# The hand-over between the passes and the last part of a transformer block's forward and backward kernel, rearranged

## The chip, the cores and the metric

The kernel runs on one core of a Trainium2 chip. The metric is the device time of one execution in microseconds (us), given as the median of several executions. Beside it stands one profiled execution, from which all rows of the profile come. The engines are TensorE (PE; PEld is its weight load), VectorE (DVE), ScalarE (ACT), GpSimd (POOL) and SyncE (SP), which only issues DMA. Each works through its own queue in order, and they wait for each other by semaphores. GpSimd and ScalarE can issue DMA too.

## The reference

One transformer block, forward and backward: layer norm, then attention with 16 heads of width 28 and a gated feed-forward part side by side, both added to the input. The kernel returns the output and the gradients of the input and the five weights.

```python
def _fwd_reference(A_x, A_wqkv, A_wo, B_x, B_w_gate, B_w_up, B_w_down):
    def _A_ref(x, wqkv, wo):
        ...
        qkv = (x @ wqkv).reshape(B, S, 3, H, Dh) ...      # q, k, v per head
        scores = jnp.einsum("bhqd,bhkd->bhqk", q, k) * (Dh ** -0.5)
        p = _softmax(scores, axis=-1)
        o = jnp.einsum("bhqk,bhkd->bhqd", p, v)
        return ... o ... @ wo
    def _B_ref(x, w_gate, w_up, w_down):
        return (_silu(x @ w_gate) * (x @ w_up)) @ w_down
    xn = _layernorm(A_x, axis=-1)
    return A_x + _A_ref(xn, A_wqkv, A_wo) + _B_ref(xn, B_w_gate, B_w_up, B_w_down)

_out, _vjp = jax.vjp(_f, A_x, A_wqkv, A_wo, B_w_gate, B_w_up, B_w_down)
_grads = _vjp(grad_out)
```

Here S is 2048 tokens, D is 448, the feed-forward width 1792; everything is bf16. Two gradients matter for the change. The gradient of `wo` (dWo, `out_3`) is, for each head, the attention output transposed times `grad_out`. The gradient of the input (`out_1`) ends in the layer norm's backward step: with g the gradient that reaches the normalised input xn, each token's result is `grad_out + rstd * (g - mean(g) - xn * mean(g * xn))`. So it needs two sums over the 448 columns of a token, of g and of g times xn, before any of its values can be written.

## The kernel before

Tokens are cut into 16 tiles of 128, heads into 4 groups of 4 (one head per 32 partitions), queries into 4 chunks of 512.

**Forward part (`slot`, L523, to L627).** 256 slots, one for each group, query chunk and key tile: two score tiles on TensorE (L535, `s_ps`, three PSUM tiles in turn), two exponentials on ScalarE (L541, `eT`). What else TensorE has to do is cut into generators, called units, which yield after each matmul with a cost; `Fillers.pump` (L57) takes a budget of such cost per slot and places units between the slots. Units with a ready slot stand in `fill.first`: `o_unit` (L394) multiplies exponentials with values and adds up in `oacc`, `mid1` (L411) transposes and divides into `od`, `mid2` (L429) makes the gradient of the attention output and a chain of small VectorE steps (L442 to L451), whose results a DMA transpose and stores on SP carry to memory. `dwo_unit` (L459) makes a group's dWo: 16 matmuls (L462), one per token tile, over the `od` of its four query chunks, a copy to `dw_o` (L467) and four stores, one per head (L470). It becomes ready six slots after a group's last chunk. For the last group there is no slot left, so `fill.finish` (L627) runs the last `o_unit`, `mid1`, `mid2` and `dwo_unit` one after the other. Its stores are issued by ScalarE, those of the other groups by SP. `sp_flush` (L171) issues stores that were held back until their transposes are under way.

**Main backward part.** 512 steps, in each: scores again (`row`, L695, tile `sb`, a single one), the exponential (`ew`, L710, `e_sb`), the product with the upstream gradient (L703, `db`; L717 on VectorE, `ds_sb`), then the sums for dK and dV (`kv`, L745, L749) one or two steps later and, four steps at a time, transposes of `ds_sb` by DMA on SP (L720) and by TensorE (L731) for dQ. Other matmuls fill in. Operands come back from memory: `load_q(g, qc)` and `load_k` (L662 on) reserve a tile and put its loads into a list with due steps (`drip`, L640). GpSimd issues them from there: `drop` (L646) sends up to a budget of bytes per step, from step 2 on, each behind a one-column copy `pace` that waits for that step's `ds_sb` (L1055); `have` (L657) sends what is wanted at once. Before the first step L672 sends the first key and query chunk; query chunks 1 to 3 and the next keys go into the list. Step 4 is the first of query chunk 1.

**The last part (from L1081).** For each of 16 token tiles, `dx_a(t)` (L1095) adds the last terms of g on TensorE (`tok`, six PSUM tiles in turn). For an odd tile it also adds the sum so far, `dxg` in SBUF, by a matmul with the identity (L1099), and ScalarE writes a bf16 copy `gs` that nobody reads, for the sum of g on the way (L1107). For an even tile VectorE adds `dxg` itself and takes the sum (L1110). Then VectorE multiplies with xn and takes the second sum (`pr`, L1113), from PSUM for odd tiles. `dx_b(t)` (L1116) scales both sums (two VectorE instructions on 128x1, L1120), makes the first half of the result on ScalarE (L1123, from PSUM for odd tiles), the second on VectorE (L1126, tile `e_sb`), adds them on GpSimd (L1128, `dx`) and stores on SP (L1129). The loop (L1146) does `dx_a(t)` and `dx_b(t - 1)` in each turn, and one unit of the list `rest`: two units of transposes of dV or dK (`dsp_unit`, L825), four of dQ (`dsq_unit`, L1138, copied by ScalarE at L1140), four of dWqkv (`dwq_unit`, L838: 16 matmuls each that need all of `dsp`, copies on ScalarE and VectorE at L844 to L847, a store on GpSimd).

The order in which a queue holds its instructions is the order in which the code emits them.

Of the kernel before, what the change touches and what calls it, by code (L numbers as in the profile page):

```python
# [8 lines left out]
ACT = mybir.ActivationFunctionType  # L9
ALU = mybir.AluOpType  # L10
AX = mybir.AxisListType
FP32 = mybir.dt.float32
BF16 = mybir.dt.bfloat16
# [4 lines left out]
D = 448  # L18
H = 16
DH = 28  # L20
F = 1792
G = 4
HP = 32
NT = S // 128
NFC = F // 128
P = 128
# [9 lines left out]
def pv(hh):  # L36
    return (hh + 2) % 4
# [50 lines left out]
def kernel(  # L88
# [23 lines left out]
    PE, DVE, ACTE, POOL, SP = nc.tensor, nc.vector, nc.scalar, nc.gpsimd, nc.sync  # L112
# [14 lines left out]
    xn_sp = xn_t[:, :NT * D].rearrange("p (t d) -> p t d", d=D)  # L127
    rstd = const.tile([P, NT], FP32)
# [16 lines left out]
    ps_s = fwd.enter_context(tc.tile_pool(name="ps_s", bufs=3, space=PSUM))  # L145
    gen = fwd.enter_context(tc.tile_pool(name="gen", bufs=2, space=PSUM))
# [24 lines left out]
    def sp_flush():  # L171
        for o, i in late:
            SP.dma_start(out=o, in_=i)
        late.clear()
# [114 lines left out]
    def run(u):  # L289
        for _ in u:  # L290
            pass
# [102 lines left out]
    def o_unit(g, qc, m, eTs):  # L394
        ps = gen.tile([P, 512], FP32, name="gen")
        for kt in range(4 * m, 4 * m + 4):
            for hh in range(4):
                r = HP * pv(hh)
                PE.matmul(ps[r:r + HP, :], lhsT=VS[g][:, kt, r:r + HP], rhs=eTs[kt][hh // 2][:, hh % 2, :],  # L399
                          start=(kt % 4 == 0), stop=(kt % 4 == 3), tile_position=(0, r), skip_group_check=True)  # L400
            if kt % 4 < 3:
                yield 216
        if m == 0:
            oacc[g, qc] = wk.tile([P, 512], FP32, name="oacc")
            DVE.tensor_copy(out=oacc[g, qc][:], in_=ps[:])
        else:
            DVE.tensor_tensor(out=oacc[g, qc][:], in0=ps[:], in1=oacc[g, qc][:], op=ALU.add)
        o_done.add((g, qc, m))
        yield 316
# [47 lines left out]
        yield 60  # L457

    def dwo_unit(g):  # L459
        ps = gen.tile([P, 512], FP32, name="gen")  # L460
        for t in range(NT):
            PE.matmul(ps[:, :D], lhsT=od[g, t // 4][0][:, 0, t % 4, :], rhs=dy_sp[:, t, :],  # L462
                      start=(t == 0), stop=(t == NT - 1))
            if t < NT - 1:
                yield 189
        o = wk.tile([P, D], BF16, name="dw_o", bufs=1)
        DVE.tensor_copy(out=o[:], in_=ps[:, :D])  # L467
        for hh in range(4):
            h = g * 4 + hh
            (ACTE if g == G - 1 else SP).dma_start(out=out_3[h * DH:(h + 1) * DH, :], in_=o[HP * pv(hh):HP * pv(hh) + DH, :])  # L470
        yield 189

    fill = Fillers()
# [45 lines left out]
    NS = G * 4 * NT  # L519
# [3 lines left out]
    def slot(i):  # L523
        nonlocal eTs
        g, qc, kt = i // 64, (i // 16) % 4, i % 16
        qsl = slice(qc * 512, (qc + 1) * 512)
        m = i - EB // 2
        if m >= 0 and m % 4 == 0:
            fill.until(lambda: (m // 64, (m // 16) % 4, (m % 16) // 4) in o_done, i)
        sp2 = []  # L530
        for hp in range(2):
            s_ps = ps_s.tile([P, 2, 512], FP32, name="s_ps")
            for j in range(2):
                r = HP * (2 * hp + j)
                PE.matmul(s_ps[:, j, :], lhsT=KK[g][r:r + HP, kt * P:(kt + 1) * P], rhs=QQ[g][r:r + HP, qsl],  # L535
                          start=True, stop=True, tile_position=(r, 0))
            sp2.append(s_ps)
        e2 = []
        for hp in range(2):
            eT = wk.tile([P, 2, 512], BF16, name="eT", bufs=EB)  # L540
            ACTE.activation(out=eT[:], in_=sp2[hp][:], func=ACT.Exp, scale=SCALE)  # L541
            e2.append(eT)
        eTs[kt] = e2
        if kt % 4 == 3:
            fill.first.append((i + 1, lambda e=dict(eTs): o_unit(g, qc, kt // 4, e)))
        if kt == 15:
            fill.first.append((i + 3, lambda: mid1(g, qc)))
            fill.first.append((i + 4, lambda: mid2(g, qc)))
            if qc == 3:
                fill.first.append((i + 6, lambda: dwo_unit(g)))  # L550
            eTs = {}
        fill.pump(FWD_NS, i)
# [19 lines left out]
    for t in range(4):  # L572
        run(T_unit(xnT, xn_t, t, t % 2 == 0, ps_s if t < 2 else None))
    DVE.tensor_reduce(out=r_ones[:],
                      in_=ident_f[:].rearrange("p (a b) -> p a b", b=HP)[:, :, 28:30],
# [4 lines left out]
    proj(1, 0, True)  # L580
    proj(0, 0)
    slot(0)
    proj(2, 0)
    norm4(1)
    T(4, 5)
    slot(1)
    T(6, 7)
    proj(1, 1)
    stats4(2)
    slot(2)  # L590
    proj(2, 1)
    slot(3)
# [31 lines left out]
    slot(15)  # L624
    for i in range(16, NS):
        slot(i)
    fill.finish()  # L627
    sp_flush()
    fwd.close()

# [9 lines left out]
    def drip(key, pieces, due):  # L640
        slow.extend((due, key, o, i) for o, i in pieces)
        slow.sort(key=lambda x: x[0])
# [14 lines left out]
    def have(*keys):  # L657
        for x in [x for x in slow if x[1] in keys]:
            slow.remove(x)
            POOL.dma_start(out=x[2], in_=x[3])  # L660

    def load_q(g, qc):  # L662
        t = qside[g, qc] = bk.tile([P, 4, 512], BF16, name="qd", bufs=5)
        drip(("q", g, qc), [(t[:, i:i + 2], QD_d[g, qc, :, i:i + 2]) for i in (0, 2)], 128 * g + 4 * qc)
# [5 lines left out]
    load_k(0, 0)  # L670
    load_q(0, 0)
    have(("k", 0, 0), ("q", 0, 0))  # L672
    for qc in range(1, 4):
        load_q(0, qc)
    load_k(0, 1)

# [232 lines left out]
    dxs = {}  # L909
# [130 lines left out]
    for k in range(NB + 12):  # L1040
        now = k
        if k < NB:
            g, hp, kc, qc, qi = steps[k]
# [40 lines left out]
    tw, wqT = dxs["tw"], dxs["wq"]  # L1084
# [5 lines left out]
    SP.dma_start(out=dy2[1][:], in_=dy_d[:, 4:8, :])  # L1090
    dy4 = bk.tile([P, 8, D], BF16, name="dsT", bufs=3)
    SP.dma_start(out=dy4[:], in_=dy_d[:, 8:16, :])
    psd, sms = {}, {}

    def dx_a(t):  # L1095
        pst = ps_b.tile([P, 512], FP32, name="tok", bufs=6)
        ps = psd[t] = pst[:, :D]
        if t % 2:
            PE.matmul(ps, lhsT=ident_f[:], rhs=dxs["g"][:, t, :], start=True, stop=False)  # L1099
        for i, (l, r) in enumerate(last):  # L1100
            PE.matmul(ps, lhsT=l[:, t * P:(t + 1) * P], rhs=r, start=(i == 0 and t % 2 == 0), stop=(i == 3))  # L1101
        sa = tw.tile([P, 1], FP32, name="sa", bufs=4)
        sb = tw.tile([P, 1], FP32, name="sb", bufs=4)
        sms[t] = (sa, sb)
        if t % 2:
            gs = tw.tile([P, D], BF16, name="gs")
            ACTE.activation(out=gs[:], in_=ps, func=ACT.Identity, accum_out=sa[:])  # L1107
        else:
            psd[t] = dxs["g"][:, t, :]
            DVE.scalar_tensor_tensor(out=psd[t], in0=ps, scalar=1.0, in1=psd[t],  # L1110
                                     op0=ALU.mult, op1=ALU.add, accum_out=sa[:])
        pr = tw.tile([P, D], BF16, name="pr")
        DVE.scalar_tensor_tensor(out=pr[:], in0=psd[t], scalar=1.0, in1=xn_sp[:, t, :],  # L1113
                                 op0=ALU.mult, op1=ALU.mult, accum_out=sb[:])

    def dx_b(t):  # L1116
        ps = psd.pop(t)
        sa, sb = sms.pop(t)
        for x in (sa, sb):
            DVE.tensor_scalar(out=x[:], in0=x[:], scalar1=rstd[:, t:t + 1], scalar2=-1.0 / D,  # L1120
                              op0=ALU.mult, op1=ALU.mult)
        t1 = tw.tile([P, D], FP32, name="t1")[:]
        ACTE.activation(out=t1, in_=ps, func=ACT.Identity, scale=rstd[:, t:t + 1], bias=sa[:])  # L1123
        t2 = bk.tile([P, 512], FP32, name="e_sb", bufs=4)[:, :D]
        dy = dy2[t // 4][:, t % 4, :] if t < 8 else dy4[:, t - 8, :]
        DVE.scalar_tensor_tensor(out=t2, in0=xn_sp[:, t, :], scalar=sb[:], in1=dy, op0=ALU.mult, op1=ALU.add)  # L1126
        dx = tw.tile([P, D], BF16, name="dx")
        POOL.tensor_tensor(out=dx[:], in0=t1, in1=t2, op=ALU.add)  # L1128
        SP.dma_start(out=out1_d[:, t, :], in_=dx[:])  # L1129

    g = G - 1
    rest = [dsp_unit(g, 2, t8, "rest") for t8 in range(2)]
# [10 lines left out]

    rest += [dsq_unit(t4, "rest") for t4 in range(4)]
    rest += [dwq_unit(g, c, "rest") for c in range(4)]
    for t in range(NT + 1):  # L1146
        if t < NT:
            dx_a(t)
        if t > 0:
            dx_b(t - 1)  # L1150
        if rest:
            for _ in rest.pop(0):
                pass
    for u in rest:
# [35 lines left out]
```

## Time and profile before

| | before |
|---|---|
| median of 6 runs | 1594.11 us |
| lowest, highest run | 1585.56, 1622.87 us |
| profiled execution | 1602.12 us |
| its span | 1600.3 us |
| busy: TensorE, VectorE, ScalarE, GpSimd | 1362.6, 1191.1, 1148.7, 653.8 us |
| granted TensorE clock, mean | 0.962 |
| forward part, main part, last part | to about 669, 669 to 1546.6, 1546.6 to 1600.3 us of the span |

The profile is of one execution; a start is counted in us from the start of its span. A row of a timeline has start, length, engine, line, operation, what is written and read, how many instructions were merged, and in brackets how long the engine was idle before and what ended that. "q" behind an engine's name is its queue: an issue of DMA, not work. In a row of windows the columns are the stretch, its length, and the busy time of PE, PEld, DVE, ACT and POOL with the number of instructions, then the granted TensorE clock as a share of full speed, the busy share of DMA and GB/s. A group's row in the page has busy time and the mean of one instruction in ns. Line numbers are those of the kernel before, unless said otherwise.

### The profile page before, as it was taken

What the parts mean: (1) busy time and instruction counts of PE and PEld (TensorE: products, weight loads), DVE (VectorE), ACT (ScalarE), POOL (GpSimd) and SP (SyncE); (2) the same over time, 40 slices, a digit from 0 to 9 for tenths busy, and PEclk for the clock granted to TensorE, in tenths of its full rate; (3) what the DMA queues carried; (4) which work ended last, traced back from release to release, by engine and by line L of the source; (5) the groups of instructions that cost most, each with busy time, mean ns of one, the idle gap of its engine ahead of it and who ended that gap; (6) DMA issues with size and microseconds to landing.
All of it is one profiled execution on the core that took longest, in us unless ns stands there. A gap on an engine that the chain in (4) does not pass through costs nothing. (4 is left out here: it accounts for less than half of the span.)

```text
span 1600.3 us, 31339 instructions
## 1 busy us (share of the span) xinstructions
PE 1362.6 (85%) x11728; PEld 550.5 (34%) x11728; DVE 1191.1 (74%) x1603; ACT 1148.7 (72%) x1320; POOL 653.8 (41%) x1095
## 2 busy tenths in 40 slices
PE   5789888879889897677789889889899898988985
PEld 2333333323333333232333333323333333333332
DVE  7576556646665665287689998879889799969986
ACT  5588878868788887466567777757677777756753
POOL 3445344343434443045345634644524346141214
PEclk9899999999999999789889999999999999999998
DMA  4978856576667656289999998999979999899851
GB/s 126 198 187 196 184 136 154 130 182 150 146 164 169 158 145 137 71 176 178 161 202 220 226 184 177 185 223 201 223 140 193 162 209 227 159 161 184 160 126 45
DMA packets 652560, 270.42 MB, mean 169 GB/s; under 512 B 598600, under 2 KB 626648, under 8 KB 652408
## 3 DMA queue, kind: packets, MB, share of 16 engines
q1 hardware_dynamic: 626496, 198.85, 65.0%
q0 software_dynamic: 24336, 69.17, 17.2%
q8 instruction: 92, 1.51, 0.4%
q10 hardware_dynamic: 1576, 0.40, 0.1%
q14 instruction: 60, 0.49, 0.1%
HBM read 63.99 MB, written 58.85 MB: 77 GB/s over the span
## 5 line engine op out<-in xcount | busy, mean ns | idle before, releaser
L717 DVE TENSOR_TENSOR ds_sb<-db,e_sb 128x1024 bf16<-128x1024 f32 x512 | 623.2, 1222 | 107.3 <-PE db L703 37.3
L710 ACT ACTIVATE e_sb<-sb 128x1024 bf16<-128x1024 f32 x512 | 524.2, 1024 | 237.9 <-PE db L703 178.1
L541 ACT ACTIVATE eT<-s_ps 128x1024 bf16<-128x1024 f32 x512 | 491.9, 1026 | 115.5 <-PE s_ps L535 114.0
L695 PE MATMUL sb<-kd,qd 32*128 32x512 bf16 x1024 | 205.2, 391 | 71.5 <-ACT e_sb L710 56.2
L703 PE MATMUL db<-kd,qd 32*128 32x512 bf16 x1024 | 204.5, 394 | 5.1 <-DVE ds_sb L717 4.7
L331 POOL TENSOR_TENSOR nn<-nn,ag 128x512 f32<-128x512 f32 x56 | 71.1, 1269 | 285.4 <-DVE ag L329 284.5
L695 PEld LDWEIGHTS <-qd 32*128 32x128 bf16 x1024 | 74.7, 91 | 257.0 <-issue 239.4
L749 PE MATMUL acc<-ds_sb,qd 128*32 128x512 bf16 x1024 | 162.0, 395 | 1.1 <-DVE ds_sb L717 1.1
L796 POOL TENSOR_TENSOR dq_acc<-dq_acc,dq_st 128x512 f32<-128x512 f32 x88 | 111.8, 1271 | 123.3 <-ACT dq_st L795 121.9
L745 PE MATMUL acc<-e_sb,qd 128*32 128x512 bf16 x1024 | 161.3, 396 | 0.0
L1055 POOL COPY pace<-ds_sb 128x1 bf16<-128x1 bf16 x287 | 54.4, 189 | 207.1 <-DVE ds_sb L717 204.8
L535 PE MATMUL s_ps<-QQ,KK 32*128 32x512 bf16 x1024 | 112.3, 391 | 12.6 <-ACT eT L541 11.7
L946 PE MATMUL genb<-wguT,dau_c 128*128 128x448 bf16 x448 | 111.1, 358 | 4.8 <-DMA dau_c<-F_d 3.6
L731 PE MATMUL db<-ident_bf,ds_sb 128*128 128x128 bf16 x1088 | 85.6, 225 | 34.2 <-DVE ds_sb L717 27.6
L370 PE MATMUL gen<-xn_t,f_sp 128*128 128x448 bf16 x448 | 98.1, 356 | 9.8 <-DVE nn L346 5.4
L731 PEld LDWEIGHTS <-ds_sb 128*128 128x128 bf16 x1088 | 72.9, 100 | 62.4 <-issue 57.6
L370 PEld LDWEIGHTS <-f_sp 128*128 128x128 bf16 x672 | 60.4, 98 | 95.3 <-issue 34.5
L732 DVE COPY dsT<-db 128x1024 bf16<-128x1024 bf16 (+1 forms) x128 | 91.5, 715 | 1.0 <-PE db L731 1.0
L781 PE MATMUL genb<-dsT,kd 128*32 128x512 bf16 x1024 | 80.8, 389 | 2.1 <-DVE qd L791 1.2
L353 PE MATMUL gen<-dyT,wT_f 128*128 128x512 bf16 x224 | 63.6, 388 | 15.5 <-DVE nn L346 15.4
L535 PEld LDWEIGHTS <-KK 32*128 32x128 bf16 x1024 | 28.1, 91 | 135.9 <-issue 135.2
L399 PE MATMUL gen<-eT,VS 128*32 128x512 bf16 x1024 | 70.6, 395 | 3.2 <-DVE nn L346 2.4
(261 smaller groups left out, 2034.5 us busy)
## 6 DMA issues: line engine op xcount, KB each, us to landing
F_d<-hda SPq DMA_DIRECT2D x56, 384.0 KB, 3.2
dau_c<-F_d POOLq DMA_DIRECT2D x56, 256.0 KB, 5.2
qd<-QD_d POOLq DMA_DIRECT2D x32, 256.0 KB, 5.0
h_c<-F_d POOLq DMA_DIRECT2D x24, 256.0 KB, 5.4
dc<-dqkvT_d POOLq DMA_DIRECT2D x12, 384.0 KB, 5.9
kd<-KD_d POOLq DMA_DIRECT2D x16, 256.0 KB, 4.9
dsT<-ds_sb SPq DMA_TRANSPOSE x248, 5.3
wT_d<-wT_f SPq DMA_DIRECT2D x14, 256.0 KB, 2.3
```

The source lines that it names most:

```text
L370: PE.matmul(ps[:, :D], lhsT=fsp[fc][:, t // 4, w, t % 4, :], rhs=rhs[:, t, :], start=(t == 0), stop=(t == NT - 1))
L535: PE.matmul(s_ps[:, j, :], lhsT=KK[g][r:r + HP, kt * P:(kt + 1) * P], rhs=QQ[g][r:r + HP, qsl], start=True, stop=True, tile_position=(r, 0))
L541: ACTE.activation(out=eT[:], in_=sp2[hp][:], func=ACT.Exp, scale=SCALE)
L695: PE.matmul(s_ps[:, j, :], lhsT=qside[g, qc][r:r + HP, 0, qi * P:(qi + 1) * P], rhs=kside[g, kc][r:r + HP, 0, :], start=True, stop=True, t ...
L703: PE.matmul(d_ps[:, j, :], lhsT=qside[g, qc][r:r + HP, 1, qi * P:(qi + 1) * P], rhs=kside[g, kc][r:r + HP, 1, :], start=True, stop=True, t ...
L710: ACTE.activation(out=est[k][:], in_=sps.pop(k)[:], func=ACT.Exp, scale=SCALE)
L717: DVE.tensor_tensor(out=ds[:, qi % 2], in0=dps.pop(k - 1)[:], in1=est[k - 1][:], op=ALU.mult)
L731: PE.transpose(ps[:, c, :], ds[:, q0 + c // 8, c // 4 % 2, (c % 4) * P:(c % 4 + 1) * P], ident_bf[:])
L745: PE.matmul(a[r:r + HP, :], lhsT=sp4[:, 1, r:r + HP], rhs=e[:, j, :], start=first, stop=last, tile_position=(0, r), skip_group_check=True)
L749: PE.matmul(a[r:r + HP, :], lhsT=sp4[:, 0, r:r + HP], rhs=ds[:, qi % 2, j, :], start=first, stop=last, tile_position=(0, r), skip_group_ch ...
L796: POOL.tensor_tensor(out=dq_acc[:, qsl], in0=dq_acc[:, qsl], in1=st[:], op=ALU.add)
L946: PE.matmul(ps[:, :D], lhsT=d[:, i // 2, i % 2, tsl], rhs=dxs["w"][:, f0 + i // 2, i % 2, :], start=(i == 0), stop=(i == n - 1))
```

## The change

Four edits.

1. The last group's `dwo_unit` is taken out of the list of fillers. After the last slot, what is ready is pumped, and then the unit runs up to the point where the last query chunk begins: 12 of its 16 matmuls. `fill.finish` then runs the last `o_unit`, `mid1` and `mid2`, and the last four matmuls, the copy and the stores follow. Its PSUM tile comes from the score tiles' pool, not from `gen`.
2. Its four stores are issued by SP, as for the other groups.
3. Query chunk 1 of the backward part is loaded at once before the first step, like chunk 0. Every later load moves up in the list.
4. In the last part all tiles keep g in `dxg` in SBUF: ScalarE writes it there for odd tiles, in place of `gs`. The two sums lie side by side in one tile `sm`, and one GpSimd instruction scales both into two further columns. A new step `dx_m` holds `pr` and that scaling. The loop runs `dx_a(t)`, `dx_m(t - 1)`, `dx_b(t - 2)`, and a unit of `rest` from turn 2 on; it has 18 turns, not 17.

```diff
     def dwo_unit(g):
-        ps = gen.tile([P, 512], FP32, name="gen")
+        ps = gen.tile([P, 512], FP32, name="gen") if g < G - 1 else ps_s.tile([P, 2, 512], FP32, name="s_ps")[:, 0, :]
         for t in range(NT):
+            if g == G - 1 and t == NT - 4:
+                yield None
             PE.matmul(ps[:, :D], lhsT=od[g, t // 4][0][:, 0, t % 4, :], rhs=dy_sp[:, t, :],
...
-            (ACTE if g == G - 1 else SP).dma_start(out=out_3[h * DH:(h + 1) * DH, :], in_=o[HP * pv(hh):HP * pv(hh) + DH, :])
+            SP.dma_start(out=out_3[h * DH:(h + 1) * DH, :], in_=o[HP * pv(hh):HP * pv(hh) + DH, :])
...
-            if qc == 3:
+            if qc == 3 and g < G - 1:
                 fill.first.append((i + 6, lambda: dwo_unit(g)))
...
+    fill.pump(1e9, NS - 2)
+    u = dwo_unit(G - 1)
+    while next(u) is not None:
+        pass
     fill.finish()
+    run(u)
     sp_flush()
...
-    for qc in range(1, 4):
+    load_q(0, 1)
+    have(("q", 0, 1))
+    for qc in range(2, 4):
         load_q(0, qc)
...
-        sa = tw.tile([P, 1], FP32, name="sa", bufs=4)
-        sb = tw.tile([P, 1], FP32, name="sb", bufs=4)
-        sms[t] = (sa, sb)
+        sm = sms[t] = tw.tile([P, 4], FP32, name="sm", bufs=4)
+        g_t = dxs["g"][:, t, :]
         if t % 2:
-            gs = tw.tile([P, D], BF16, name="gs")
-            ACTE.activation(out=gs[:], in_=ps, func=ACT.Identity, accum_out=sa[:])
+            ACTE.activation(out=g_t, in_=ps, func=ACT.Identity, accum_out=sm[:, 0:1])
         else:
-            psd[t] = dxs["g"][:, t, :]
-            DVE.scalar_tensor_tensor(out=psd[t], in0=ps, scalar=1.0, in1=psd[t],
-                                     op0=ALU.mult, op1=ALU.add, accum_out=sa[:])
+            DVE.scalar_tensor_tensor(out=g_t, in0=ps, scalar=1.0, in1=g_t,
+                                     op0=ALU.mult, op1=ALU.add, accum_out=sm[:, 0:1])
+
+    def dx_m(t):
+        sm = sms[t]
         pr = tw.tile([P, D], BF16, name="pr")
-        DVE.scalar_tensor_tensor(out=pr[:], in0=psd[t], scalar=1.0, in1=xn_sp[:, t, :],
-                                 op0=ALU.mult, op1=ALU.mult, accum_out=sb[:])
+        DVE.scalar_tensor_tensor(out=pr[:], in0=dxs["g"][:, t, :], scalar=1.0, in1=xn_sp[:, t, :],
+                                 op0=ALU.mult, op1=ALU.mult, accum_out=sm[:, 1:2])
+        POOL.tensor_scalar(out=sm[:, 2:4], in0=sm[:, 0:2], scalar1=rstd[:, t:t + 1], scalar2=-1.0 / D,
+                           op0=ALU.mult, op1=ALU.mult)
 
     def dx_b(t):
...
-        for x in (sa, sb):
-            DVE.tensor_scalar(out=x[:], in0=x[:], scalar1=rstd[:, t:t + 1], scalar2=-1.0 / D,
-                              op0=ALU.mult, op1=ALU.mult)
...
-        ACTE.activation(out=t1, in_=ps, func=ACT.Identity, scale=rstd[:, t:t + 1], bias=sa[:])
+        ACTE.activation(out=t1, in_=dxs["g"][:, t, :], func=ACT.Identity, scale=rstd[:, t:t + 1], bias=sm[:, 2:3])
...
-    for t in range(NT + 1):
+    for t in range(NT + 2):
         if t < NT:
             dx_a(t)
-        if t > 0:
-            dx_b(t - 1)
-        if rest:
+        if 0 < t <= NT:
+            dx_m(t - 1)
+        if t > 1:
+            dx_b(t - 2)
+        if rest and t > 1:
             for _ in rest.pop(0):
                 pass
```

More of the change, by code (lines that the diff above doesn't have):

```diff
@@ L1092 @@
     SP.dma_start(out=dy4[:], in_=dy_d[:, 8:16, :])
-    psd, sms = {}, {}
+    sms = {}
     def dx_a(t):
         pst = ps_b.tile([P, 512], FP32, name="tok", bufs=6)
-        ps = psd[t] = pst[:, :D]
+        ps = pst[:, :D]
         if t % 2:
@@ L1116, in dx_b @@
     def dx_b(t):
-        ps = psd.pop(t)
-        sa, sb = sms.pop(t)
-        for x in (sa, sb):
-            DVE.tensor_scalar(out=x[:], in0=x[:], scalar1=rstd[:, t:t + 1], scalar2=-1.0 / D,
-                              op0=ALU.mult, op1=ALU.mult)
+        sm = sms.pop(t)
         t1 = tw.tile([P, D], FP32, name="t1")[:]
-        ACTE.activation(out=t1, in_=ps, func=ACT.Identity, scale=rstd[:, t:t + 1], bias=sa[:])
+        ACTE.activation(out=t1, in_=dxs["g"][:, t, :], func=ACT.Identity, scale=rstd[:, t:t + 1], bias=sm[:, 2:3])
@@ L1124, in dx_b @@
         t2 = bk.tile([P, 512], FP32, name="e_sb", bufs=4)[:, :D]
         dy = dy2[t // 4][:, t % 4, :] if t < 8 else dy4[:, t - 8, :]
-        DVE.scalar_tensor_tensor(out=t2, in0=xn_sp[:, t, :], scalar=sb[:], in1=dy, op0=ALU.mult, op1=ALU.add)
+        DVE.scalar_tensor_tensor(out=t2, in0=xn_sp[:, t, :], scalar=sm[:, 3:4], in1=dy, op0=ALU.mult, op1=ALU.add)
         dx = tw.tile([P, D], BF16, name="dx")
```

## The prediction

> **What bounds the kernel now.** I read the busy table in 40 slices first, to see which stretches the change can reach, then the timeline around the two places that it edits, then the waits there.
>
> ```profile
> ## 2 busy tenths in 40 slices
> PE   5789888879889897677789889889899898988985
> ...
> DVE  7576556646665665287689998879889799969986
> ...
> PEclk9899999999999999789889999999999999999998
> ```
>
> A slice is 40 us. TensorE and VectorE share the limit almost everywhere; the exceptions are the hand-over from forward to backward pass (slice 17: VectorE at 2, clock 7) and the last 54 us. The change edits just these two. The loop of 512 steps between them keeps its instructions.
>
> The hand-over, from the timeline of all engines:
>
> ```profile
> 664.51 4.52 PE L462 MATMUL gen<-dy_t,od 128*128 128x448 bf16 x16
> 667.27 0.20 DVE L451 CAST od<-dl 128x16 bf16<-128x16 f32 x1
> 668.96 0.39 PE L695 MATMUL sb<-kd,qd 32*128 32x512 bf16 x2
> 669.06 0.62 DVE L467 CAST dw_o<-gen 128x448 bf16<-128x448 f32 x1 [1.59 <-PE gen L462]
> 669.72 2.07 ACTq L470 DMA_DIRECT2D out_dram<-dw_o  x4
> 671.84 1.02 ACT L710 ACTIVATE e_sb<-sb 128x1024 bf16<-128x1024 f32 x1 [11.39 <-DMA out_dram<-dw_o]
> 676.70 0.54 POOL L651 DMA_DIRECT2D qd<-QD_d  x1
> 680.74 0.60 PE L695 MATMUL sb<-kd,qd 32*128 32x512 bf16 x2 [3.02 <-DMA qd<-QD_d]
> ```
>
> The last dWo (L462) stands in front of the first backward scores (L695); ScalarE's first exponential waits behind four dWo stores on its own queue; and the fifth step, the first of query chunk 1, waits 3 us for a load that was issued only 4 us before.
>
> The tail: busy time of the stretch in which dwq runs (PE 12.95 of 13 us, the column after the length), then rows of VectorE, and rows of GpSimd:
>
> ```profile
> 1563.00:1576.00 13.00, 12.95 (x71) 7.28 (x71) 8.56 (x30) 5.62 (x17) 6.96 (x8) 1.00 0.20 57
> ```
>
> ```profile
> 1581.52 1.17 DVE L1113 SCALAR_TENSOR_TENSOR pr<-dxg,xn_t 128x448 bf16<-128x448 f32 x1
> ...
> 1583.06 0.69 DVE L1126 SCALAR_TENSOR_TENSOR e_sb<-xn_t,sb,dsT 128x448 f32<-128x448 bf16 x1
> 1584.20 0.62 DVE L1113 SCALAR_TENSOR_TENSOR pr<-tok,xn_t 128x448 bf16<-128x448 f32 x1 [0.46 <-ACT gs L1107]
> ```
>
> ```profile
> 1581.07 1.13 POOL L1128 TENSOR_TENSOR dx<-t_20962,e_sb 128x448 bf16<-128x448 f32 x1 [1.00 <-ACT t_20962 L1123]
> 1583.88 1.13 POOL L1128 TENSOR_TENSOR dx<-t_20981,e_sb 128x448 bf16<-128x448 f32 x1 [1.67 <-DVE e_sb L1126]
> ...
> 1592.69 1.12 POOL L1128 TENSOR_TENSOR dx<-t_21051,e_sb 128x448 bf16<-128x448 f32 x1 [0.61 <-DVE e_sb L1126]
> ```
>
> So the tail is bound by TensorE from 1563 to 1576 and by VectorE after. A pair of tiles takes 4.94 us (dxg starts at 1580.86 and 1585.80). See in the rows that the product `pr` takes 1.17 us when it reads `dxg` from SBUF while GpSimd adds `dx` (1581.07 to 1582.20, and `pr` ends 0.49 later), but 0.62 when it reads PSUM beside the same add.
>
> **Hand-over, part by part.** *dWo split.* Its first 12 matmuls now follow the last scores of the forward pass, the other 4 follow mid2. They write a score tile of PSUM, which is free when the third-last exponential ends (six of them from 654.84 to 660.44, so 658.6). The row gives 0.37 each at half clock, 4.5 us, to 663.1; the attention output unit then takes 1.9 and ends at 665.0, where it ended at 661.1 before: 3.9 lost there. The Trainium skill says in "TensorE: Matmul & The Clock Gate", section "What's actually happening", that a busy window of some 3.4 us brings the full clock back. The trace agrees in part: the granted clock steps at 657.0, 667.1 and 674.0, three and two such windows apart, so one falls at 663.7; but the window before it was only some 70% busy and stayed slow. By the row alone the unit ends at 665.0; by the rule the matmuls now fill the window from 660.3 to 663.7, and it ends at 664.4. I take 664.4.
>
> From there: oacc 0.69, transposes and od at full clock 1.75, then VectorE's mid2 chain of 2.72 (L442 to L451), 669.6. *The added wait:* the first backward scores reuse the PSUM of dWo, so TensorE waits for the dw_o copy, which VectorE does after that whole chain, and everything of the backward pass is queued behind this on TensorE. Copy 0.62, scores 0.39: exponential at 670.65 instead of 671.84, **1.2 gained**. Bounds: half clock throughout 672.5, 0.7 lost; full clock from 658.6 on 668.1, 3.7 gained.
>
> *Stores from ScalarE to SP.* ScalarE's 2.07 us go, already in that sum. On SP they are 4 x some 0.5 us, of which two wait for the transpose of od and for an earlier store. Queued behind them: the stores of OT and QD for the last group, needed hundreds of us later, and the first transpose of ds, which goes from 676.4 to some 676.5. Its reader is dq at step 13, some 20 us later: cost nothing. Without that cover it would be about 1 us.
>
> *Second query chunk.* Two issues of 0.54 us join those at 633 to 635, when GpSimd has nothing until its memset at 653.5: nothing. The fifth step then starts one step (1.72) after the fourth, at 677.86 by before's clock, not at 680.74: **2.9 gained**. What is late next: chunk 2, whose issues move up two places to steps 2 and 3 and which is needed at step 8, 10 us later; then the wait for kd at 701.6, 0.5 us, which falls too. Bounds 2.0 and 3.4.
>
> **Tail, part by part.** *Removed:* two tensor_scalar of 0.12 per tile on VectorE, with gaps around them, and `gs`; ScalarE writes `dxg` for the same 0.55. *Added:* one GpSimd tensor_scalar per tile, nearest row 0.23 (L196, 128x4), hidden under `e_sb`; one more turn of the loop. *Moved:* `pr` one tile behind, results two; the units of `rest` start two turns later.
>
> TensorE first: its dwq chain starts when ScalarE has copied the fourth dsq, at 1563.0 before. Now that copy stands behind t1 of tile 5; I walk VectorE's turns to its `pr` at 1560.6, the small product and t1 0.3 and 0.75, the copy 0.5: 1562.2. The chain is as long as before (12.3: rest of one unit, three units of 2.6, tiles of 0.75, 1.5 and 1.5), so dwq's copies end at 1575.5, not 1576.4. But by then results up to tile 9 are out, not 8. Left are 6 `e_sb`, 5 `pr`, 2 `dxg`.
>
> *The new contention.* The odd `pr` now reads two SBUF operands as well. Its own row says 625 ns, eight times of eight. Against this change speaks "SBUF — State Buffer", section "Who interferes with whom": a VectorE instruction with two SBUF inputs and a GpSimd one that reads SBUF exclude each other, and the earlier one holds the ports to its end. A turn then is add 1.13, signal 0.13, `pr` 0.50, `e_sb` 0.61 = 2.37, with `dxg` hidden; by the row it is 1.25 or 1.9. I take the rule, since all of the even `pr` that meet an add show it. Sum: first turn free of an add 1.9, four of 2.35 (9.4), last `e_sb` behind an add 1.75, its own add 1.26: 1575.5 + 14.3 = 1589.8, against 1593.81: **4.0 gained**. By the row 1585.5, where GpSimd's own adds set the end: 8.3. If the small product takes a turn at the ports too, 0.28 more per turn: 1592.4, 1.4. The last 6.5 us (store, end) stay.
>
> **Sum.** 1.2 + 2.9 + 4.0 = 8.1 us. The profiled execution took 1602.1 (span 1600.3 and 1.8 around it): 1594.0. That execution lies 8 us above the median of the runs, 1594.1; the sum holds there too: **1586.0**. Ends of the unknowns: 2.7 to 15.4 gained, 1591 to 1579.
>
> **Rivals.** *The ports cost no more than before:* VectorE slips into GpSimd's gaps and the tail gains 8.3; 1581.7. For it: in the turns without dxg VectorE is ready 0.13 before GpSimd. Against: the last `e_sb`, 1.39 us under an add. 0.20.
> *The hand-over's gain is lost on the way:* between 740 and 800 VectorE waits 13.2 us for transposes of ds, so DMA may set the pace there; only the tail's 4.0 stays, 1590.1. Against: the loads are paced by the steps and move with them. 0.20.
> *The tail goes slower:* one mechanism, GpSimd's adds and products taking strict turns at the ports with `pr` and `e_sb`: 1.13 + 0.13 + 0.50 + 0.28 + 0.13 + 0.61 = 2.8 to 2.9 in every turn. 17 turns from 1548.2 and 3.0 to drain end at 1600.5, 6.7 later than before; less 4.1 from the hand-over, 2.6 slower: 1596.7. It decides from 2.75 a turn ((1593.8 + 4.1 - 1548.2 - 3.0) / 17). For it: the table of waits shows GpSimd waiting on `e_sb` in 13 of 16 tiles, so both are in lockstep. Against: in TensorE's stretch there is slack for it. 0.17.
> *My forecast:* 0.43.
>
> Range 1577 to 1598: from the best end to the slower rival, a little wider as six runs between 1585.6 and 1622.9 leave their median uncertain by some us. A measurement of this kernel can tell about 1% (16 us) from no change. That much faster needs every term at its best end and luck of the runs: 0.2. Slower by that needs more than the rival gives: 0.1. Between: 0.7.
>
> **What would show it.** Right: no wait of L695 for the load of chunk 1; exponential L719 0 to 3 us earlier after the output unit; all `pr` beside an add at 1.1 to 1.2; dwq's copies within 1 us of 1575.5, shifted by the hand-over; turns of 2.3 to 2.4 at the end. Wrong: turns over 2.75; odd `pr` at 0.62; half clock through the whole hand-over; or a pass between that is longer by more than the two ends give, which I have no term for.

## The result and the profile after

The changed kernel takes 1578.33 us (median of 10 runs, 1569.18 to 1601.5); the kernel before, run beside it on the same chip, 1604.58 us (20 runs, 1582.03 to 1637.89). The ratio is 0.988, with an interval from 0.9825 to 0.9935: about 19 us gained, somewhere from 10 to 28. All ratios here leave out the runs over 1.5% above the fastest of their kernel, so they differ from the quotients of the medians; the profiled runs of the change, of chunk 1 alone and of the change without edit 3 are such longer ones. The forecast was 1586.0 us against 1594.1, a ratio of 0.995. The time lies in the range given, close to its better end of 1577; the gain is larger than the sum said. In part this is luck: the kernel before had a higher median in this comparison, and 0.988 of the forecast's own 1594.1 would be 1575, just outside the range.

The profiled execution of the changed kernel took 1599.76 us, span 1598.0, against 1602.1 and 1600.3 before. So the two spans say little, and the two traces are compared place by place. I measure each from an event inside it. Hand-over: from the start of the last L383 copy on VectorE (of dW, before the hand-over begins; called the anchor) to the first backward exponential and to the scores of the fifth step. Last part: from the first `dxg` to the end of the last add. The pass between is what lies between these two. The rows that these lengths start from and end with, as far as they are not shown elsewhere, first of before, then of after:

```profile
653.48 0.62 DVE L383 CAST dw_o_7936<-gen 128x448 bf16<-128x448 f32 x1 [2.84 <-PE gen L370]
1547.54 0.62 DVE L1110 SCALAR_TENSOR_TENSOR dxg<-tok,dxg 128x448 f32<-128x448 f32 x1
```

```profile
656.05 0.62 DVE L383 CAST dw_o_7936<-gen 128x448 bf16<-128x448 f32 x1 [2.83 <-PE gen L370]
1549.21 0.62 DVE L1116 SCALAR_TENSOR_TENSOR dxg<-tok,dxg 128x448 f32<-128x448 f32 x1
1590.34 1.13 POOL L1135 TENSOR_TENSOR dx<-t_21008,e_sb 128x448 bf16<-128x448 f32 x1 [0.62 <-DVE e_sb L1133]
```

| from ... to | before | after | gained | forecast |
|---|---|---|---|---|
| anchor to first backward exponential | 18.36 | 16.51 | 1.85 | 1.2 |
| that exponential to the fifth step's scores | 8.90 | 6.23 | 2.67 | 2.9 |
| last part | 46.27 | 42.26 | 4.01 | 4.0 |
| the pass between | 866.8 | 870.4 | -3.6 | no term |

The three edited places give 8.5 us, where the sum had 8.1. The busy table of after, in 40 slices:

```profile
## 2 busy tenths in 40 slices
PE   5789889878899899678989789878799888899985
...
DVE  6576666546656666289999888778789889889986
...
PEclk9899999999999999879999999999899999999998
```

Slice 17, the hand-over, still has VectorE at 2; its clock is 8 instead of 7, and the slice after it has 7. The hand-over in the timeline of all engines, after:

```profile
657.41 5.61 ACT L543 ACTIVATE eT<-s_ps 128x1024 bf16<-128x1024 f32 x6 [1.55 <-PE s_ps L537]
661.23 3.60 PE L464 MATMUL s_ps<-dy_t,od 128*128 128x448 bf16 x12 [0.53 <-ACT eT L543]
664.76 1.51 PE L399 MATMUL gen<-eT,VS 128*32 128x512 bf16 x16
668.81 0.93 PE L464 MATMUL s_ps<-dy_t,od 128*128 128x448 bf16 x4 [0.19 <-DVE od L422]
671.46 0.62 DVE L469 CAST dw_o<-s_ps 128x448 bf16<-128x448 f32 x1
672.13 0.39 PE L704 MATMUL sb<-kd,qd 32*128 32x512 bf16 x2 [2.39 <-DVE dw_o L469]
672.56 1.02 ACT L719 ACTIVATE e_sb<-sb 128x1024 bf16<-128x1024 f32 x1 [9.54 <-PE sb L704]
675.90 2.09 SPq L472 DMA_DIRECT2D out_dram<-dw_o  x4
678.79 0.61 PE L704 MATMUL sb<-kd,qd 32*128 32x512 bf16 x2
```

See the 12 matmuls ahead of the attention output unit (L399), the scores waiting 2.39 us for the copy of dw_o (this is the added wait), and the exponential starting 0.04 us after these scores end. The fifth step's scores (678.79) wait for no load. The four stores, 2.09 us of issue, now stand on SP.

The last part: busy time in the stretch of TensorE's dwq work (TensorE is busy all 13.00 us, at full clock), then VectorE and GpSimd behind it.

```profile
1565.00:1578.00 13.00, 13.00 (x71) 7.30 (x70) 8.48 (x25) 5.93 (x17) 9.68 (x12) 1.00 0.25 73
```

```profile
1577.44 0.21 DVE L855 CAST dwq_o<-rest 64x56 bf16<-64x56 f32 x1 [2.73 <-ACT dwq_o L854]
1582.25 1.28 DVE L1122 SCALAR_TENSOR_TENSOR pr<-dxg,xn_t 128x448 bf16<-128x448 f32 x1
1583.46 0.68 DVE L1133 SCALAR_TENSOR_TENSOR e_sb<-xn_t,sm,dsT 128x448 f32<-128x448 bf16 x1
1584.06 0.61 DVE L1122 SCALAR_TENSOR_TENSOR pr<-dxg,xn_t 128x448 bf16<-128x448 f32 x1
1584.76 1.54 DVE L1133 SCALAR_TENSOR_TENSOR e_sb<-xn_t,sm,dsT 128x448 f32<-128x448 bf16 x1
1586.22 0.61 DVE L1122 SCALAR_TENSOR_TENSOR pr<-dxg,xn_t 128x448 bf16<-128x448 f32 x1
1586.92 1.54 DVE L1133 SCALAR_TENSOR_TENSOR e_sb<-xn_t,sm,dsT 128x448 f32<-128x448 bf16 x1
```

```profile
1583.64 1.08 POOL L1124 TENSOR_SCALAR sm<-sm,rstd 128x2 f32<-128x2 f32 x1 [0.59 <-DVE pr L1122]
1584.69 1.13 POOL L1135 TENSOR_TENSOR dx<-t_20973,e_sb 128x448 bf16<-128x448 f32 x1
1585.80 1.09 POOL L1124 TENSOR_SCALAR sm<-sm,rstd 128x2 f32<-128x2 f32 x1
1586.85 1.12 POOL L1135 TENSOR_TENSOR dx<-t_20991,e_sb 128x448 bf16<-128x448 f32 x1
```

In the last two turns shown, `pr` takes 0.61 and `e_sb` 1.54: it stands under the add that starts beside it (1584.69 and 1586.85) and ends some 0.5 after that add. In the turn with a `dxg` ahead it is `pr` that waits (1.28) and `e_sb` that doesn't (0.68). Once per turn VectorE is held behind an add, at one pass or the other. The ends of these `e_sb` lie 2.16 us apart (start and length of a row added up: 1584.14 and 1586.30), and again 2.16 from there.

### The profile page after: what moved, and what is told of

Read it like the earlier page. It is cut to its first block, busy times and chain, and to the rows that moved or that the text cites. A ratio compares the mean times of both kernels' runs of the same rounds, so it can differ in the third digit from the quotient of the medians.

```text
span 1598.0 us, 31319 instructions
## 1 busy us (share of the span) xinstructions
PE 1361.3 (85%) x11728; PEld 549.2 (34%) x11728; DVE 1190.6 (75%) x1571; ACT 1149.0 (72%) x1320; POOL 665.2 (42%) x1108
## 4 chain that ended last, share of the span: by engine, by line
PE 45%; DVE 22%; DMA 13%; ACT 12%; issue 5%; POOL 2%; DVEq 0%; SPq 0%; POOLq 0%; ACTq 0%
ACT e_sb L719 10%; DMA dsT<-ds_sb 8%; PE gen L370 8%; DVE ds_sb L726 8%; PE sb L704 7%; PE s_ps L537 4%; PE db L740 3%; PE acc L754 2%; PE gen L399 2%; PE genb L906 2%; PE gen L316 2%; DVE hda L345 2%; PE genb L955 2%; DVE nn L346 2%; PE genb L847 2%
## 5 line engine op out<-in xcount | busy, mean ns | idle before, releaser
L537 PE MATMUL s_ps<-QQ,KK 32*128 32x512 bf16 x1024 | 111.4, 390 | 12.3 <-ACT eT L543 11.2
L955 PE MATMUL genb<-wguT,dau_c 128*128 128x448 bf16 x448 | 115.6, 370 | 4.5 <-DMA dau_c<-F_d 4.2
L353 PE MATMUL gen<-dyT,wT_f 128*128 128x512 bf16 x224 | 63.5, 388 | 18.6 <-DVE nn L346 18.5
L332 POOL TENSOR_TENSOR nn<-nn,tt 128x512 f32<-128x512 f32 x56 | 71.0, 1268 | 4.4
```

Source lines behind the costliest of these rows:

```text
L955: PE.matmul(ps[:, :D], lhsT=d[:, i // 2, i % 2, tsl], rhs=dxs["w"][:, f0 + i // 2, i % 2, :], start=(i == 0), stop=(i == n - 1))
```

## The experiments

The medians of whole kernels have intervals of half a per cent and more to each side, 8 us, as large as what a part of the change should give. So each kernel was also profiled, in one execution, and the lengths of the stages above carry the verdicts. In the diffs, `-` is the kernel that the heading names as the start.

**The last part alone** (start: before).

```diff
+        sm = sms[t] = tw.tile([P, 4], FP32, name="sm", bufs=4)
...
-    for t in range(NT + 1):
+    for t in range(NT + 2):
...
-        if rest:
+        if rest and t > 1:
```

> Edit 4 alone; the hand-over is that of the kernel before. Stages of the profile, used for all runs: hand-over, from the second of the last two casts of dW (the last matmuls of the fillers) to the scores of backward step 4, 27.3 us before and 22.7 in the changed kernel; last part, from the first dxg sum to the end of the last add, 46.3 and 42.3. My theory (the two ends give all of it, each by itself): hand-over 27 us as before, last part 42.3, and 4 us (0.25%) off the time. Rival (the main part of 512 steps also gets shorter, by the hand-over's doing): the same for this run, so it sets the baseline: ratio 0.997 to 0.998. Were the last part the cause of the larger measured gain, the ratio would be 0.99 here.

1597.16 us (12 runs), ratio 0.993 (0.9887 to 0.9973); 0.997 to 0.998 was expected. The last part took 42.25 us, as in the full change, and the hand-over 17.66 to the exponential and 26.47 to the fifth step, near before's. The 4.0 us belong to this part and to nothing else.

**The hand-over alone, all three edits of it** (start: changed kernel, with before's last part).

```diff
-    for t in range(NT + 2):
+    for t in range(NT + 1):
...
-        if rest and t > 1:
+        if rest:
```

> Edits 1 to 3 alone; the last part is that of the kernel before. My theory: hand-over 22.7 us, last part 46.3, 4.5 us off, ratio 0.997. Rival: the main part gets shorter too, because all later loads have moved up in the list and fewer of them meet the transposes of ds: 10 to 15 us off, ratio 0.99 to 0.993, with a shorter main part in the profile as well (866 us before).

1586.32 us (12 runs), ratio 0.9902 (0.9862 to 0.9941). Last part 46.27, as before; 14.87 us to the exponential and 20.89 to the fifth step. The pass between took 846.2 us, 20.6 less than before's, in this execution. So in this execution the hand-over's gain isn't given back on the way, and the time falls by more than it. The expected ratio of 0.997 was missed; what came is the rival's value, a main part that is shorter as well.

**The stores back on ScalarE** (start: changed kernel).

```diff
-            SP.dma_start(out=out_3[h * DH:(h + 1) * DH, :], in_=o[HP * pv(hh):HP * pv(hh) + DH, :])
+            (ACTE if g == G - 1 else SP).dma_start(out=out_3[h * DH:(h + 1) * DH, :], in_=o[HP * pv(hh):HP * pv(hh) + DH, :])
```

> The changed kernel with the last dWo's four stores back on ScalarE (edit 2 undone). My theory: ScalarE's first exponential waits for them again; the fourth waits for the transpose of od, issued after the dWo copy here, so it comes some 3 us later than in the changed kernel (16.5 us after the last cast there, 19 to 20 here), which is worse than the kernel before (18.4), since the copy is now later against the scores. Hand-over 25.5 to 26. Rival (SP's queue is what counts, the stores delay the first transpose of ds and with it dq): hand-over as in the changed kernel, but steps 13 to 20 earlier by 2 us.

1578.21 us (4 runs), ratio 0.9842 (0.9786 to 0.9898). Timeline of its hand-over:

```profile
672.79 1.91 ACTq L472 DMA_DIRECT2D out_dram<-dw_o  x4
672.81 0.39 PE L704 MATMUL sb<-kd,qd 32*128 32x512 bf16 x2 [2.39 <-DVE dw_o L469]
674.80 1.02 ACT L719 ACTIVATE e_sb<-sb 128x1024 bf16<-128x1024 f32 x1 [9.47 <-DMA out_dram<-dw_o]
```

The scores end at 673.20, the exponential starts at 674.80: the stores on ScalarE cost 1.6 us. The total was 16.43 us to the exponential, not the 19 to 20 expected; the 12 matmuls took 2.43 us here and 3.60 in the changed kernel. In the hand-over alone, with the stores on SP, they ran as fast (2.43), and there the exponential came after 14.87: 1.6 earlier again, so the 1.6 stands in the whole hand-over too. The rival's steps 13 to 20 did not come earlier: from the exponential to step 16 it is 28.9 us with the stores on either queue.

**dWo unsplit, the stores on SP and chunk 1 at once kept** (start: changed kernel).

```diff
-        ps = gen.tile([P, 512], FP32, name="gen") if g < G - 1 else ps_s.tile([P, 2, 512], FP32, name="s_ps")[:, 0, :]
+        ps = gen.tile([P, 512], FP32, name="gen")
...
-            if qc == 3 and g < G - 1:
+            if qc == 3:
```

> The changed kernel with dWo in one piece after mid2 (edit 1 undone), stores on SP, chunk 1 early. My theory: the first scores follow dWo directly as before, and wait neither for the dWo copy nor for VectorE's chain; the exponential is no longer held by stores. By before's row 669.35 against 671.84 it comes 2.5 us earlier than before, that is 15.9 after the last cast, where the split version has 16.5: the split gives nothing, -0.6 to +0.6. Rival (the split is what shortens the hand-over): 18 us or more to the exponential.

1582.99 us (4 runs), ratio 0.9869 (0.9812 to 0.9927). Timeline:

```profile
667.09 3.80 PE L462 MATMUL gen<-dy_t,od 128*128 128x448 bf16 x16
670.82 0.39 PE L697 MATMUL sb<-kd,qd 32*128 32x512 bf16 x2
671.25 1.02 ACT L712 ACTIVATE e_sb<-sb 128x1024 bf16<-128x1024 f32 x1 [8.22 <-PE sb L697]
```

The scores follow the 16 matmuls at once and wait for no copy. 15.19 us to the exponential: less than the changed kernel's 16.51, a little more than the 14.87 of the hand-over alone, which has the split. All six kernels with the split give 14.87 to 17.54. The three without it that keep the stores on ScalarE (before, the last part alone, chunk 1 alone) give 17.66 to 18.37. Taking some 2 us of stores off these, an estimate from the rows, leaves 15.7 to 16.4. Nothing here shows a gain by the split, and the stores' move is enough to account for what the hand-over won ahead of the exponential. Each kernel has one profile, and the spread among those with the split is as large as the difference looked for.

**Chunk 1 at once, alone** (start: before).

```diff
-    for qc in range(1, 4):
+    load_q(0, 1)
+    have(("q", 0, 1))
+    for qc in range(2, 4):
```

> Only edit 3 in the kernel before. So far the main part's steps 32 to 80 took 97 us before and 90 with edit 4 alone, but 76 to 79 with edits 1 to 3; that was not forecast. Theory A (the list of loads stands two pieces further on at each step, so its loads come to lie elsewhere against the transposes of ds): 76 to 79 here too, step 4 some 2.7 us earlier, ratio 0.99. Rival B (the stores of dWo on SP, or the earlier start, do it): 90 to 97 here, and only 2.7 us off, ratio 0.998.

1597.04 us (6 runs) against 1608.7 beside it; ratio 0.9855 (0.9792 to 0.9919), from three runs. From the exponential to the fifth step 24.38 - 18.37 = 6.01 us, against 8.90 before: 2.9 gained. In its timeline the stores still hold the first exponential:

```profile
672.70 0.39 PE L697 MATMUL sb<-kd,qd 32*128 32x512 bf16 x2
673.46 2.28 ACTq L470 DMA_DIRECT2D out_dram<-dw_o  x4
675.79 1.02 ACT L712 ACTIVATE e_sb<-sb 128x1024 bf16<-128x1024 f32 x1 [11.40 <-DMA out_dram<-dw_o]
```

**The change without this edit** (start: changed kernel; the same lines the other way round).

```diff
-    load_q(0, 1)
-    have(("q", 0, 1))
-    for qc in range(2, 4):
+    for qc in range(1, 4):
```

> The changed kernel without edit 3. Theory A: steps 32 to 80 take 90 to 97 us again, step 4 waits 2.7 us for its load again, and what is left is the last part's 4.0 and the hand-over's 1 to 3: ratio 0.993 to 0.996. Rival B: 76 to 79 us, ratio 0.99 or less.

1599.18 us (6 runs) against the same 1608.7; ratio 0.9865 (0.9799 to 0.9932), again from three runs. From the exponential to the fifth step 26.32 - 17.54 = 8.78 us: the wait is back. Its whole-kernel ratio is no worse than that of the full change, where 0.993 to 0.996 was expected. So the whole-kernel times can't place the gain that goes beyond the three places.

**Chunk 1 at once, but charged to the loads that follow** (start: changed kernel). The list of loads is released by a credit that grows with the steps; the added line takes chunk 1's bytes off it, so that the other loads keep their steps.

```diff
     have(("q", 0, 1))
+    credit = -2 * P * 1024 * 2
```

> The changed kernel with chunk 1 loaded at once, but its two pieces charged to the list's budget (the credit starts at minus 524288 bytes), so every later load is sent at the same step as before. It tells two readings of A apart. A1 (the place of the later loads against the steps matters): steps 32 to 80 take 90 to 97 us, and only the 2.7 us at step 4 stay. A2 (chunk 1 itself matters: without its wait, the first steps and their transposes start in another rhythm): 76 to 79 us.

1591.01 us (4 runs), ratio 0.9887 (0.9828 to 0.9945).

The disputed stretch is steps 32 to 80 of the backward pass, where the pass before and the passes with edit 3 part. The length of these 48 steps in one profile of each kernel, by the starts of the `ds_sb` passes; beside the whole pass stand VectorE's waits in it for the DMA transposes of `ds_sb`:

| kernel | chunk 1 at once | steps 32 to 80, us | whole pass between, us | waits for transposes in it, us |
|---|---|---|---|---|
| before | no | 96 | 866.8 | 30.6 |
| last part alone | no | 90 | 865.7 | 23.9 |
| change without this edit | no | 83 | 868.2 | 28.0 |
| change | yes | 76 | 870.4 | 36.2 |
| hand-over alone | yes | 76 | 846.2 | 12.1 |
| stores back | yes | 77 | 844.2 | 12.3 |
| unsplit | yes | 79 | 859.0 | 20.6 |
| chunk 1 alone | yes | 77 | 864.8 | 28.1 |
| chunk 1 charged | yes | 80 | 862.0 | 19.3 |
| small product on ScalarE (below) | yes | 78 | 848.8 | 12.7 |

Waits in the stretch of steps 32 to 80, of before and of the hand-over alone (total, times, longest):

```profile
DVE ds_sb L717 <- DMA dsT<-ds_sb: 13.2, 7, 4.5
```

```profile
DVE ds_sb L726 <- DMA dsT<-ds_sb: 0.6, 1, 0.6
```

And steps 48 to 64 of both in the busy-time view (the last two columns are DMA's busy share and GB/s):

```profile
760.50:793.40 32.90, 25.38 (x232) 9.73 (x232) 23.67 (x24) 18.81 (x21) 15.19 (x28) 0.91 1.15 170
```

```profile
751.10:777.10 26.00, 23.78 (x236) 9.42 (x232) 23.64 (x25) 18.65 (x22) 12.51 (x22) 1.00 1.17 213
```

VectorE does the same work in both (23.67 and 23.64 us); before, it waits for transposes of ds. The DMA engines move about the same in both, 5.6 and 5.5 MB (length times GB/s), and count as equally busy, but take 32.9 us for it instead of 26.0.

All seven kernels that load chunk 1 at once need 76 to 80 us, the three others 83 to 96; if it made no difference, the three longest of ten would be these three once in 120 drawings. But the stretch was picked from the first six profiles. Of the four made after that, chunk 1 alone gave the expected 77, while the change without edit 3 gave 83, nearer to 80 than to the 90 to 97 expected. The charged kernel's 80 says that the earlier place of the later loads isn't needed for most of it. Why the transposes come through sooner is not settled.

And this saving does not reach the end dependably: the whole pass spreads over 844.2 to 870.4 with the edit; the mean of the seven is 856.5, of the three 866.9 (852.0 and 866.3 without the three longer executions named above). What the passes differ by is for the most part the same kind of wait. Over the whole pass, of before, of the change and of the hand-over alone:

```profile
DVE ds_sb L717 <- DMA dsT<-ds_sb: 30.6, 16, 4.5
```

```profile
DVE ds_sb L726 <- DMA dsT<-ds_sb: 36.2, 15, 5.4
```

```profile
DVE ds_sb L726 <- DMA dsT<-ds_sb: 12.1, 6, 4.9
```

The change's pass is 24.2 us longer than that of the hand-over alone, though the steps are the same code, and its waits for transposes are 24.1 us longer. Before's pass is 20.6 us longer than that one, its waits 18.5. The change's profile has none of these waits in steps 32 to 80; they fall later. Less these waits, the ten passes lie between 831.9 and 842.7, without a clear order by edit 3.

**The small product on ScalarE, and the dsq and dwq blocks from turn 0** (start: changed kernel).

```diff
-        POOL.tensor_scalar(out=sm[:, 2:4], in0=sm[:, 0:2], scalar1=rstd[:, t:t + 1], scalar2=-1.0 / D,
-                           op0=ALU.mult, op1=ALU.mult)
...
+    nrstd = tw.tile([P, NT], FP32, name="nrstd", bufs=1)
+    DVE.tensor_scalar(out=nrstd[:], in0=rstd[:], scalar1=-1.0 / D, scalar2=None, op0=ALU.mult)
...
-        if rest and t > 1:
+        if 0 < t <= NT:
+            sm = sms[t - 1]
+            ACTE.activation(out=sm[:, 2:4], in_=sm[:, 0:2], func=ACT.Copy, scale=nrstd[:, t - 1:t])
+        if rest:
```

> The changed kernel with two edits in the last part: ScalarE scales the two sums (128x2, after t1 in each turn), not GpSimd, and the units of rest start at turn 0 as before the change. In the changed kernel the small GpSimd product takes 0.63 to 1.08 us, as it waits for VectorE at the ports, and VectorE waits 2.7 us for the last dwq. My theory (the ports, then TensorE's chain, set the last part): the chain starts some 3 us earlier, VectorE's waits for dwq go, turns stay near 2.2 us as add, pr and e_sb still exclude each other: last part 39 to 40 us against 42.3. Rival (the end is set by something else, such as GpSimd's adds or ScalarE, which now has more to do): 42 us or more.

1582.39 us (6 runs), ratio 0.9845 (0.9802 to 0.9888). The last part took 42.17 us against 42.26: nothing gained, a miss. VectorE near its end, with the last of the dwq copies first:

```profile
1556.68 0.21 DVE L855 CAST dwq_o<-rest 64x56 bf16<-64x56 f32 x1 [2.73 <-ACT dwq_o L854]
...
1565.74 1.28 DVE L1124 SCALAR_TENSOR_TENSOR pr<-dxg,xn_t 128x448 bf16<-128x448 f32 x1
1566.95 0.68 DVE L1133 SCALAR_TENSOR_TENSOR e_sb<-xn_t,sm,dsT 128x448 f32<-128x448 bf16 x1
1567.55 0.61 DVE L1124 SCALAR_TENSOR_TENSOR pr<-dxg,xn_t 128x448 bf16<-128x448 f32 x1
1568.09 1.55 DVE L1133 SCALAR_TENSOR_TENSOR e_sb<-xn_t,sm,dsT 128x448 f32<-128x448 bf16 x1
```

```profile
1565.41 1.13 POOL L1135 TENSOR_TENSOR dx<-t,e_sb 128x448 bf16<-128x448 f32 x1 [0.62 <-DVE e_sb L1133]
1567.76 1.39 POOL L1135 TENSOR_TENSOR dx<-t,e_sb 128x448 bf16<-128x448 f32 x1 [1.22 <-DVE e_sb L1133]
1569.77 1.39 POOL L1135 TENSOR_TENSOR dx<-t,e_sb 128x448 bf16<-128x448 f32 x1 [0.62 <-DVE e_sb L1133]
```

The passes keep their 1.28 and 1.55 though GpSimd does only its adds now, which wait for `e_sb`: so the small product isn't needed to hold VectorE, and each held pass stands beside an add. The dwq copies ended 24.9 us after the first `dxg`, 3.7 earlier than in the changed kernel (28.6), but 8 adds were still to come instead of 6. Two turns of some 2 us took the gain. Also VectorE still waits 2.73 us for the last dwq block. Here the blocks' place only trades turns ahead of them for turns behind them. These two edits were made together; an effect of each with opposite sign isn't excluded.

No kernel of these is clearly better than the changed one: their intervals overlap.

## Why the prediction was right, and where it was short

**Hand-over, dWo and the exponential.** Forecast 1.2, measured 1.85. The 12 matmuls started 5.2 us after the anchor (5.1 in the forecast), and the output unit ended 10.2 after it, where the choice of the clock rule over the half-clock row gave 10.9. The rule held in one point. This stretch of after is busy throughout at half clock, and the full clock follows it (1.00 from 666 to 668):

```profile
662.30:665.70 3.40, 3.40 (x20) 1.16 (x21) 0.00 (x0) 0.71 (x1) 0.00 (x0) 0.50 0.00 0
```

But the forecast had half clock from the first matmul on, and in the profile the clock was full until 662.3; so the matmuls took 3.60 us and not the 4.5 of the row. Where the steps of the clock fall is luck: in other executions the same matmuls took 2.43 to 4.64 us. The added wait showed as forecast, 2.39 us for the dw_o copy behind VectorE's chain.

The one figure of 1.2 also hides two parts of opposite sign. By the forecast's own rows the exponential before could have started at 669.35, when the scores ended, so the stores' move is worth 2.5 us in it and the split costs 1.3. The runs show 1.6 for the stores; of the split they show no gain, and a cost of this size fits them but isn't shown.

**The stores on SP.** Costed at nothing. They took 2.09 us there from 675.90, and the first transpose of ds goes behind them, at 678.98. That is 22.9 us after the anchor, as before the change; the forecast had 0.1 more. Its readers did not wait in the hand-over. With the stores on either queue the fifth step came 6.2 us after the exponential (22.67 - 16.43 and 22.74 - 16.51). Right.

**Chunk 1.** Forecast 2.9; 2.67 in the change, 2.9 alone, and the wait is back without the edit. Right.

**The last part.** Forecast 4.0, measured 4.01, and in all six kernels that have this last part alike (42.2 to 42.3 us); but two terms were off and cancel, so that the agreement is closer than the sum deserves. The dwq copies ended 28.6 us after the first `dxg`, not 28.0. What came after took 13.7, not 14.3: the turns were 2.36, 2.16 and 2.16 us, not 2.35 each. The forecast let every `pr` wait for an add; in fact the wait changes place between `pr` and `e_sb`. That a VectorE pass with two inputs in SBUF is held by a GpSimd add that reads SBUF is what "SBUF — State Buffer" of the Trainium skill says in the section "Who interferes with whom", and all traces agree, 1.28 or 1.54 us beside 0.61 and 0.68. The row-only value (8.3 us gained) is refuted. That the ports are the reason stays argued: a kernel without the adds wasn't tried. The new GpSimd product was costed at 0.23 and hidden; it took 0.27 with VectorE away, and 0.35 to 1.09 in the last six turns. It seems to have been hidden all the same: with it taken away, and the blocks begun earlier, the last part was 0.1 us shorter. One bound of the sum doesn't come out: 0.28 more in each of the six turns left would be 1.7 us, not the 2.6 that lie between 1589.8 and 1592.4.

**The rivals.** "The ports cost no more" wanted a last part of some 38 us; it took 42.26. "Strict turns" decided from 2.75 us a turn; the turns were 2.16 to 2.36. "The hand-over's gain is lost on the way" wanted a ratio near that of the last part alone (0.993); the hand-over alone gave 0.9902, but the two intervals overlap. In the change's own profile most of it was lost: the pass is 3.6 us longer, of 4.5 gained. On the average of the profiles it wasn't, as the passes with chunk 1 at once are shorter.

**What failed.** The sum stopped at the two ends: "a pass between that is longer by more than the two ends give, which I have no term for". A term was missing, with the opposite sign. The places gave 8.5 us and the kernel gained about 19; the 8.1 of the forecast lies outside the interval of 10 to 28, and 19 is beyond its best end of 15.4. A gain of over 1% was given a chance of 0.2. The nearest candidate is in the trace that the forecast read: VectorE's 13.2 us of waits for transposes between 740 and 800, used there only as an argument for a rival. With chunk 1 loaded at once steps 32 to 80 need 76 to 80 us, not 83 to 96. Means of the pass (866.9 and 856.5) differ by 10.4, which with 8.5 makes 18.9. That this is the missing part isn't shown: the change's own profile has the longest pass of all, 870.4, and the kernel without edit 3 gains as much as the one with it, within their intervals. The length of the pass in a given execution goes with VectorE's waits for the transposes, 12.1 to 36.2 us in all; what makes these transposes late, and whether edit 3 makes them so less often, stays open.

## What to carry to other kernels

Before a wait at the start of a long loop is costed at its own length, look at what else shares its queue and its loads farther on: here the waits of a later stretch, 3.3 to 13.2 us, were gone or down to at most 1.9 in every kernel with the earlier load, though the saving did not last to the end of the loop in each execution. In a drain where two engines share operands in SBUF, cost each turn as one pass of the one held by one of the other, whichever pass it falls on, and don't count on a gain from moving the small work between engines as long as the number of turns behind the last block grows with it; the one trial here gave 0.1 us. Where one part is worth a quarter of a per cent, take its length from an event just before it to one just after; the whole kernel's time can't tell it.

## What the runs showed of the hardware

A 128x2 product on GpSimd took 0.27 us with VectorE idle and up to 1.09 beside VectorE's passes over SBUF. The add, of 1.13 us in the changed kernel, is 1.39 in some turns when it no longer has that product ahead of it: the wait is on both engines.

The same 12 matmuls took 2.43, 3.60 and 4.64 us in three kernels with the same code there (stores back, the change, the change without edit 3), at a mean granted clock of 1.00, 0.65 and 0.50. So where the clock steps down moves the hand-over by up to 2 us, as much as the edits do.

The same DMA busy share (1.15 and 1.17 in the last columns) went with 170 and 213 GB/s. In these two stretches the share didn't tell how much could still be moved.

The steps of the backward pass are the same code in every kernel, but its length spread over 26 us, and VectorE's waits for DMA transposes over 24 (12.1 to 36.2).
